# Decode attention mixed with a squared-ReLU MLP: TensorE's rounds 0 to 11 in one nest of two loops, the MLP's turn behind it, and a first w2 block loaded as 121 and 7 rows

## The chip, the cores and the metric

The kernel runs on one core of a Trainium2 chip. The metric is the device time of one execution in microseconds; lower is better. Engines are named as in the profile: PE is TensorE (PEld its weight loads), DVE VectorE, ACT ScalarE, POOL GpSimd, SP SyncE. SPq and ACTq are the instructions of SP and ACT that issue DMAs.

## What is computed

For two batch rows x (2 x 1 x 448) the program mixes an attention block over a long cache and an MLP by a learned gate. All arrays are float32.

```python
q = (x @ wq).reshape(B, Sq, H, Dh)              # H = 16 heads, Dh = 256
scores = einsum("bhqd,bhkd->bhqk", q, k_cache) * Dh ** -0.5     # Sk = 4096
a = (softmax(scores) @ v_cache).reshape(B, Sq, H * Dh) @ wo
h = x @ w1 + b1                                 # 448 -> 1792
b = relu(h) ** 2 @ w2 + b2                      # 1792 -> 448
g = sigmoid((x * gate_w).sum(-1))
out = g * a + (1 - g) * b
```

The two caches hold 2 x 16 x 4096 x 256 values each, 268 MB together, and every value is read once.

## The kernel before

**Rounds.** The work is cut into 16 rounds. A round i takes one batch row and two heads, so it loads 8,388,608 bytes of K and as many of V, each as a tile of 128 partitions by 64 x 256 values (partitions 0 to 63 one head, 64 to 127 the other). K alternates between two tiles, kp0 and kp1 (round i uses number i % 2). V has one tile, vp. In a round

- DVE multiplies the K tile in place by the query, half a tile at a time, and sums the rows (`times_q` L404 and `row_sums` L409, together `rest`, L413): four instructions;
- `maximum` (L420): DVE takes a maximum per partition (m), PE spreads it over the partitions by a matmul (mt), and DVE reduces that to the negated maximum per head (nb, L431, the first line of `softmax`);
- ACT writes the exponentials to pw and their sums to rs (L438);
- `values` (L466): PE multiplies pw by the V tile in 64 matmul instructions and accumulates in PSUM (po);
- `make_q` (L375) prepares a query two rounds ahead: PE spreads a row of qs, ACT copies it. `pick` (L383) has ACT choose the next row.

**Units.** Four rounds make a unit (L262). Behind units 0, 1 and 2 stand `sums` (L453, PE adds rs over partitions), `norm` (L458, three small DVE instructions), `turn_wide` (L483: twice two ACT copies that spread po four times, and 16 PE instructions), four ACT copies to oTw, and `project` (L521): PE multiplies oTw by the unit's 1.8 MB of wo, which `load_wo` fetched into the tile wo.

**Order.** The order on every engine is the order in which the program calls `op`; an instruction waits on semaphores for what it reads and overwrites (`Flow.op`, L46). Nothing overtakes on an engine. SP issues nearly all loads, in this order in the looped rounds: V of round i, K of round i + 2, and after each unit's last round wo. A load waits until the tile that it overwrites has been read, and SP waits with it. In rounds 0 to 11 PE's instructions are written as three loops of four passes, one for each unit (L573 to L597); since a loop's waits must be the same in each pass, they use tokens (`take`, `give`), semaphores that are counted down again. The end of each unit and rounds 12 to 15 are written out.

**After the loops** (L599 to L608) comes round 12 with the order changed: SP issues K of round 14, V of round 12, and, once DVE's `rest` of round 13 has read kp1, K of round 15. PE's `values` of round 12 stand behind `maximum` of round 13. V of round 13 waits for those. V of round 14 goes into kp0, V of round 15 into vp in three pieces, and then w2 into the low columns of kp1 in five pieces, cut at columns 2, 8, 11 and 13 of 14 (W2_CUTS, L192; `load_w2`, L540). The last w2 piece is the last load.

**The MLP.** x @ w1 is done at the start, into the PSUM bank ph; ACT copies it to the tile shared at once (L396). `ffn_turn` (L550, PE, 28 matmuls of 64 columns) and `ffn_square` (L557, five small DVE instructions) stand in round 0, the second behind DVE's `rest` of round 1. hT, their result, is used first at the very end (`late_w2`, L545).

Of the kernel before, what the change touches and what calls it, by code (L numbers as in the profile page):

```python
# [23 lines left out]
class Flow:  # L24
# [7 lines left out]
    def __init__(self, nc):  # L32
        self.nc = nc
        self.eng = {PE: nc.tensor, ACT: nc.scalar, DVE: nc.vector, POOL: nc.gpsimd, SP: nc.sync}
        self.order = {e: [] for e in self.eng}
        self.ops = {}
        self.know = {e: {} for e in self.eng}
        self.seen = {}
        self.tokens = {}
        self.body, self.at, self.passes = None, 0, 0  # L40

# [4 lines left out]
    def op(self, eng, fn, r=(), w=(), give=None, take=(), dma=None):  # L46
        proc = dma or eng
        looped = eng == PE and self.body is not None
        o = Op(proc, eng, fn, give, looped)
# [38 lines left out]
        if looped:  # L88
            if self.passes == 1:
                self.body.append(o)  # L90
            else:
                first = self.body[self.at]
# [11 lines left out]

    def loop(self):
        self.body, self.passes = [], 0

    def next_pass(self):
        assert self.passes < 2 or self.at == len(self.body)
        self.passes += 1  # L110
        self.at = 0

    def end_loop(self, slot=None):
        assert self.at == len(self.body)
        self.order[PE].append((self.passes, self.body, slot))
        self.body = None

    def emit(self):
# [36 lines left out]
        for eng in (POOL, DVE, ACT, SP, PE):  # L155
            for o in self.order[eng]:
                if isinstance(o, Op):
                    one(o)
                else:
                    passes, body, slot = o  # L160
                    with nc.Fori(0, passes, engines=bass.OrderedEngineSet([TYPES[PE]]),
                                 head_slot=None if slot is None else {TYPES[PE]: slot}):
                        for p in body:
                            one(p)
            if eng == SP:
                nums = sorted(s.num for s in sems.values())
                assert nums == list(range(nums[0], nums[0] + len(nums)))
                nc.sync.sem_clear(range(nums[0], nums[0] + len(nums)))


def gated_mix_kernel(nc, x, k_cache, v_cache, wq, wo, w1, b1, w2, b2, gate_w, out):
# [19 lines left out]
    DQ = D // 4  # L191
    W2_CUTS = (2, 8, 11, 13)  # L192
    V_CUTS = (32, 56)
    LEAD = 4
    HJ = HG * DH // P
# [23 lines left out]
    eo = sb("eo", P, 2)  # L219
    m16 = sb("m16", P, 4 * HG)  # L220
    xT = sb("xT", P, 2, XC, 2, B)
    z = sb("z", B, 1)
# [83 lines left out]
    def vec(fn, r, w, give=None):  # L306
# [12 lines left out]
    vec(lambda: v_.tensor_reduce(m16, ident.rearrange("p (r k) -> p k r", r=4)[:, :4 * HG, :], axis=AX.X, op=ALU.add),  # L319
        ["ident"], ["m16"])  # L320

    xr = start_at[:, 4 * D:].rearrange("b (k r s) -> b k r s", k=XC, s=2)
# [51 lines left out]
    def make_q(i, token=False):  # L374
        c = sel if token else col(i)  # L375
        op(PE, mms([(pq[k * PH:(k + 1) * PH, :DH], c.to_broadcast([P, PH]), qs[:, k * DH:(k + 1) * DH], True, True)
                    for k in range(2)]), r=["qs", "sel" if token else "ident"], w=["pq"], take=["q"] if token else ())
        t = q_t[i % 3]
        q_of[i] = t
        op(ACT, lambda: s_.activation(t, pq[:, :DH], AF.Copy), r=["pq"], w=[f"q{i % 3}"])  # L380

    def pick(i):
        c = col(i)  # L383
        op(ACT, lambda: s_.activation(sel, c, AF.Copy), r=["ident"], w=["sel"], give="q")

# [6 lines left out]

    h_sb = shared[:2 * B, :F // 2]
    op(PE, times_x(ph, w1_t, D, FB // 2), r=["xT", place(vp, 0, D * F // P)], w=["ph"])
    for k in range(FB // 2):
        op(ACT, lambda k=k: s_.activation(h_sb[:, k * D:(k + 1) * D], ph[32 * k:32 * k + 2 * B, :D], AF.Copy),  # L396
           r=["ph"], w=[("shared", k * D, (k + 1) * D)])
    load_k(1)
# [20 lines left out]
    def maximum(i, token=False):  # L419
        s = s_t[i % 2]  # L420
        vec(lambda: v_.tensor_reduce(m, s, axis=AX.X, op=ALU.max), [f"s{i % 2}"], ["m"], give="m" if token else None)
        op(PE, mms([(mt[k * PH:(k + 1) * PH, :PH], m.to_broadcast([P, PH]), ident[:, k * PH:(k + 1) * PH], True, True)
                    for k in range(2)]), r=["m", "ident"], w=["mt"], take=["m"] if token else ())

# [3 lines left out]
    def softmax(i):  # L428
        b, n = rounds[i]
        s, nb, rs, pw = s_t[i % 2], nb_t[i % 2], None, pwt[buf(i)]  # L430
        vec(lambda: v_.tensor_reduce(nb, mt[:, :PH], axis=AX.X, op=ALU.max, negate=True), ["mt"], [f"nb{i % 2}"])  # L431
        u, k = unit_of[2 * n]
        rs = rs_t[u % 2]

        def part(e):
# [3 lines left out]
                                          bias=nb[at], accum_out=rs[at, c:c + 1]),  # L439
               r=[f"s{i % 2}", f"nb{i % 2}"], w=[(f"pw{buf(i)}", 2 * c, 2 * c + 2), (f"rs{u % 2}", c, c + 1)],  # L440
               give="pw" if e and i < LOOPED else None)

# [3 lines left out]
    def clear(i):  # L446
# [4 lines left out]
           w=[("pw0", 2 * (B * (k + e) + b), 2 * (B * (k + e) + b) + 2) for e in range(2)])  # L451

    def sums(u):  # L453
        n = B * len(units[u])
        op(PE, mms([(sm[:, :n], ones_pp, rs_t[u % 2][:, :n], True, True)]), r=["ones", f"rs{u % 2}"], w=["sm"])

# [23 lines left out]

    o_w = shared.rearrange("r (s j k p) -> r s j k p", s=2, j=HJ // 2, k=HG)

    def turn_wide(u):  # L483
        ptv = sm[:, :HJ * HG * B].rearrange("p (j c) -> p j c", c=HG * B)
        po, rl = po_t[0], rl_t[u % 2]
        pv = po.rearrange("r (s p j) -> r s j p", s=2, j=HJ)
        for lo in range(0, HJ, HJ // 2):
            for s in range(2):
                op(ACT, lambda s=s, lo=lo: s_.activation(o_w[:, s], pv[:, s, lo:lo + HJ // 2].unsqueeze(2).to_broadcast([P, HJ // 2, HG, HP]),  # L489
                                              AF.Copy), r=["po0"], w=[("shared", s * HN // 2, (s + 1) * HN // 2)])  # L490
            ov = o_w.rearrange("r s j k p -> r s j (k p)")
            op(PE, mms([(ptv[:, lo + j, :], ov[:, s, j, :], rl[:, :, s], s == 0, s == 1)
                        for j in range(HJ // 2) for s in range(2)]), r=["shared", f"rl{u % 2}"], w=["sm"])
        if u < NG - 2:
            op(ACT, lambda: s_.activation(po, zero.to_broadcast([P, 512]), AF.Copy), r=["zero"], w=["po0"])
        for k in range(HG):
            at = slice(k * HP, (k + 1) * HP)
            op(ACT, lambda k=k, at=at: s_.activation(oTw[at], ptv[at, :, B * k:B * k + B], AF.Copy), r=["sm"], w=[("oTw", k, k + 1)])  # L498

# [15 lines left out]
    def load_wo(u):  # L515
        if u < NG - 1:
            load(SP, "wo", wo_t, wo_g[u], ["wo"])
# [172 lines left out]
```

## Time and profile before

| | |
|---|---|
| time, median of 3 runs | 677.68 us (677.6 to 677.97) |
| the profiled execution, time | 677.82 us |
| the profiled execution, span from first to last instruction | 676.5 us |
| mean granted clock of PE | 0.662 |
| DVE busy | 570.2 us (84%) |
| PE busy | 245.4 us (36%) |
| ACT busy | 42.3 us (6%) |
| read from HBM | 289.56 MB |
| DMA busy, each fortieth of the span but the last | 90% or more |

The profile is one execution. Its page gives each engine's busy time, a row of forty equal slices, the DMA queues, the chain of work that ended last, and the costliest groups of instructions with what ended the idle time in front of them. The timeline lists instructions with their start in us from the span's start, their duration, their engine, output and inputs, and, in brackets, how long the engine had been idle and what released it. 1.3 us of the measured time lie outside the span.

### The profile page before, as it was taken

The page shows a single profiled execution, that of the slowest core. Times are in us where ns is not written, and L with a number is a line of the kernel's source. Part 1 is how long each engine was busy: PE and PEld are TensorE (multiplying, and loading weights), DVE is VectorE, ACT ScalarE, POOL GpSimd, SP SyncE. Part 2 cuts the span into 40 slices and gives each one's busy share as a digit, 9 for nine tenths or more (in the row PEclk, how much of TensorE's full clock was granted, in tenths as well). Part 3 has the DMA queues.
Part 4 walks back from the last instruction along what each step waited for, and adds up shares of the span by engine and source line. Part 5 has one row for each costly group of instructions (what it writes and reads, how often), then busy time and mean ns, then how long its engine had stood idle before and what let it go on. Part 6 is the DMA issues. An engine that isn't in the chain of part 4 may idle for free.

```text
span 676.5 us, 3789 instructions
## 1 busy us (share of the span) xinstructions
PE 245.4 (36%) x1658; PEld 83.3 (12%) x1658; DVE 570.2 (84%) x143; ACT 42.3 (6%) x141; POOL 0.7 (0%) x6
## 2 busy tenths in 40 slices
PE   2522350502305761140505456050411580412476
PEld 1100210100001410010101411010100140100122
DVE  3069999999999895979979896897979899999920
ACT  0001000010100201010000201000010110000000
POOL 0000000000000000000000000000000000000000
PEclk9957585655758577585756678575665765675889
DMA  9999999999999999999999999999999999999997
GB/s 381 426 438 435 435 434 434 434 434 434 434 434 434 419 435 434 434 434 434 434 434 434 457 431 434 434 434 434 430 434 430 401 460 434 434 434 434 392 439 304
DMA packets 7062, 289.71 MB, mean 428 GB/s; under 512 B 902, under 2 KB 1036, under 8 KB 1932
## 3 DMA queue, kind: packets, MB, share of 16 engines
q1 hardware_dynamic: 6880, 289.54, 99.3%
q8 instruction: 8, 0.13, 0.1%
q10 hardware_dynamic: 172, 0.02, 0.0%
q14 instruction: 2, 0.02, 0.0%
HBM read 289.56 MB, written 0.01 MB: 428 GB/s over the span
## 4 chain that ended last, share of the span: by engine, by line
DMA 48%; DVE 31%; PE 3%; SPq 1%; issue 0%; DVEq 0%
DMA kp<-in_A_k_cache_dram 32%; DVE s L409 15%; DVE kp L404 15%; DMA vp<-in_A_v_cache_dram 11%; DMA kp<-in_B_w_dram 5%; PE po L333 3%; SPq L254 1%; PE fin L333 0%; PE mt L333 0%; DVE shared L660 0%; DVEq L147 0%; DVE nb L431 0%
## 5 line engine op out<-in xcount | busy, mean ns | idle before, releaser
L404 DVE TENSOR_TENSOR kp<-kp,q 128x8192 f32<-128x8192 f32 (+2 forms) x34 | 278.2, 8183 | 57.6 <-DMA kp<-in_A_k_cache_dram 57.6
L409 DVE TENSOR_REDUCE s<-kp 128x32 f32<-128x8192 f32 x32 | 278.0, 8686 | 1.1
L333 PE MATMUL po<-vp,pw 128*16 128x512 f32 (+1 forms) x960 | 135.8, 728 | 233.0 <-PEq L145 208.9
L333 PEld LDWEIGHTS po<-vp,pw 128*16 128x16 f32 (+1 forms) x960 | 31.1, 110 | 333.5 <-issue 307.3
L333 PE MATMUL mt<-ident,m 128*64 128x64 f32 x64 | 7.3, 318 | 141.3 <-PEq L145 87.4
L333 PE MATMUL sm<-rl,shared 128*128 128x8 f32 (+1 forms) x112 | 23.6, 347 | 9.2 <-ACT shared L489 8.1
L333 PE MATMUL acc<-wo,oTw 128*2 128x448 f32 x48 | 24.8, 683 | 2.5 <-ACT oTw L498 2.5
L333 PEld LDWEIGHTS sm<-rl,shared 128*128 128x128 f32 x112 | 23.0, 311 | 10.8 <-DVE rl L462 4.6
L450 ACT ACTIVATE pw<-zero 128x128 f32<-128x128 f32 x12 | 3.7, 312 | 325.5 <-PE po L333 325.5
L333 PEld LDWEIGHTS mt<-ident,m 128*64 128x64 f32 x64 | 4.8, 191 | 155.0 <-issue 99.0
L438 ACT ACTIVATE pw<-s,nb 64x64 f32<-64x64 f32 x32 | 11.1, 348 | 169.8 <-DVE nb L431 169.6
L660 DVE COPY shared<-fin 128x112 f32<-128x112 f32 x1 | 0.3, 275 | 20.8 <-PE fin L333 20.8
L333 PE MATMUL ph<-vp,xT 128*4 128x448 f32 x28 | 8.2, 759 | 15.6 <-DMA vp<-in_B_w_dram 15.6
L333 PE MATMUL po<-kp,pw 128*8 128x512 f32 x64 | 9.4, 744 | 8.8 <-DMA kp<-in_A_v_cache_dram 8.8
L333 PE MATMUL pq<-qs,sel 128*64 128x256 f32 x48 | 12.3, 594 | 0.0
L431 DVE TENSOR_REDUCE nb<-mt 128x1 f32<-128x64 f32 x16 | 3.6, 224 | 9.8 <-PE mt L333 9.8
L333 PE MATMUL po<-vp,xT 128*4 128x512 f32 x56 | 8.7, 787 | 4.9 <-DMA vp<-in_A_wq_dram 4.9
L460 DVE RECIPROCAL rc<-sm 128x8 f32<-128x8 f32 (+1 forms) x5 | 1.0, 196 | 7.7 <-PE sm L333 7.7
L380 ACT ACTIVATE q<-pq 128x256 f32<-128x256 f32 x16 | 6.1, 383 | 21.0 <-PE pq L333 20.7
L489 ACT ACTIVATE shared<-po 128x512 f32<-128x512 f32 x12 | 6.5, 591 | 11.4 <-PE sm L333 11.4
L333 PEld LDWEIGHTS acc<-wo,oTw 128*2 128x2 f32 x48 | 4.5, 98 | 20.6 <-issue 17.8
L438 ACT ACTIVATION_READ_ACCUMULATOR pw<-s,nb 64x1 f32 x32 | 5.9, 184 | 0.0
(65 smaller groups left out, 66.2 us busy)
## 6 DMA issues: line engine op xcount, KB each, us to landing
vp<-in_A_wq_dram SPq DMA_DIRECT2D x1, 7168.0 KB, 19.4
wo<-in_A_wo_dram SPq DMA_DIRECT2D x4, 1792.0 KB, 45.2
vp<-in_A_v_cache_dram SPq DMA_DIRECT2D x1, 4096.0 KB, 24.8
vp<-in_B_w_dram SPq DMA_DIRECT2D x1, 3136.0 KB, 18.0
vp<-in_A_v_cache_dram SPq DMA_DIRECT2D x1, 3072.0 KB, 31.7
kp<-in_B_w_dram SPq DMA_DIRECT2D x1, 1344.0 KB, 37.1
vp<-in_A_v_cache_dram SPq DMA_DIRECT2D x1, 1024.0 KB, 33.7
kp<-in_B_w_dram SPq DMA_DIRECT2D x2, 448.0 KB, 33.5
```

The lines of the kernel that those rows point to most:

```text
L254: op(eng, lambda: e.dma_start(dst, src), r=r, w=w, dma=sem, give=give)
L333: i = t_.matmul(out_, lhsT, rhs, start=start, stop=stop, skip_group_check=True)
L380: op(ACT, lambda: s_.activation(t, pq[:, :DH], AF.Copy), r=["pq"], w=[f"q{i % 3}"])
L404: vec(lambda: v_.tensor_tensor(kt, kt, q.unsqueeze(1).to_broadcast([P, hi - lo, DH]), op=ALU.mult), at + [f"q{i % 3}"], at)
L409: vec(lambda: v_.tensor_reduce(s[:, at], rows(t)[:, at, :], axis=AX.X, op=ALU.add), [place(t, half * HALF, (half + 1) * HALF)], [(f"s{i % ...
L431: vec(lambda: v_.tensor_reduce(nb, mt[:, :PH], axis=AX.X, op=ALU.max, negate=True), ["mt"], [f"nb{i % 2}"])
L438: op(ACT, lambda: s_.activation(pw[at, :, 2 * c:2 * c + 2], s[at].rearrange("p (m s) -> p m s", s=2), AF.Exp, bias=nb[at], accum_out=rs[at ...
L450: op(ACT, lambda: s_.activation(at, zero.unsqueeze(2).unsqueeze(3).to_broadcast([P, NK // 2, 2, 2]), AF.Copy), r=["zero"], w=[("pw0", 2 * ...
L460: vec(lambda: v_.reciprocal(c, sm[:, :B * n].rearrange("p (k b) -> p k b", b=B)), ["sm"], ["rc"])
L489: op(ACT, lambda s=s, lo=lo: s_.activation(o_w[:, s], pv[:, s, lo:lo + HJ // 2].unsqueeze(2).to_broadcast([P, HJ // 2, HG, HP]), AF.Copy), ...
L660: vec(lambda: v_.tensor_copy(y4, fin[:, :DQ]), ["fin"], [("shared", 0, DQ)])
```

## The change

The change replaces PE's three loops by one nest: an outer loop of three units, in it an inner loop of four rounds, then the end of the unit. So the end of a unit is now written once, and its waits have become tokens as well:

- `make_q` is one matmul of 128 columns instead of two of 64, with two ACT copies of 64 partitions instead of one of 128; `maximum` is one matmul instead of two, and `softmax` reduces mt in two DVE instructions of 64 partitions. The token for pw is now given by `pick`, behind the exponentials and the copies of q.
- `hold_sums` (new): ACT copies rs to rs_w before `sums` reads it.
- `norm_wide` (new) takes the place of `norm` for units 0 to 2: DVE also folds the two halves of po into a tile o (128 x 256) and works out rw from m8, a new constant.
- `turn_wide` has one ACT copy of 1024 columns and 8 matmuls, where it had four copies of 512 and 16 matmuls.
- `project` takes tokens of ACT's last copy to oTw and of wo's load.
- The MLP: ACT's copies of ph, `ffn_turn` and `ffn_square` are moved from the start and from rounds 0 and 1 to the place behind the nest, ahead of the loads and DVE's `rest` of round 13. ACT's two copies write each value twice, into the tile wo (it was the tile shared), and `ffn_turn` has 14 matmuls of 128 columns where it had 28 of 64.
- w2 is cut at columns 1, 8, 11 and 13, and the first piece is loaded as two, rows 0 to 120 and rows 121 to 127.

```diff
-    W2_CUTS = (2, 8, 11, 13)
+    W2_CUTS = (1, 8, 11, 13)
     V_CUTS = (32, 56)
+    LOW_ROWS = 121
...
     def make_q(i, token=False):
         c = sel if token else col(i)
-        op(PE, mms([(pq[k * PH:(k + 1) * PH, :DH], c.to_broadcast([P, PH]), qs[:, k * DH:(k + 1) * DH], True, True)
-                    for k in range(2)]), r=["qs", "sel" if token else "ident"], w=["pq"], take=["q"] if token else ())
+        op(PE, mms([(pq[:, :2 * DH], c.to_broadcast([P, P]), qs, True, True)]), r=["qs", "sel" if token else "ident"], w=["pq"])
...
-        op(ACT, lambda: s_.activation(t, pq[:, :DH], AF.Copy), r=["pq"], w=[f"q{i % 3}"])
+        for k in range(2):
+            at = slice(k * PH, (k + 1) * PH)
+            op(ACT, lambda k=k, at=at: s_.activation(t[at], pq[at, k * DH:(k + 1) * DH], AF.Copy), r=["pq"], w=[(f"q{i % 3}", k, k + 1)])
...
-    h_sb = shared[:2 * B, :F // 2]
     op(PE, times_x(ph, w1_t, D, FB // 2), r=["xT", place(vp, 0, D * F // P)], w=["ph"])
-    for k in range(FB // 2):
-        op(ACT, lambda k=k: s_.activation(h_sb[:, k * D:(k + 1) * D], ph[32 * k:32 * k + 2 * B, :D], AF.Copy),
-           r=["ph"], w=[("shared", k * D, (k + 1) * D)])
     load_k(1)
...
+    def norm_wide(u):
+        c = rc[:, :HG]
+        po = po_t[0]
+        vec(lambda: v_.reciprocal(c, sm[:, :B * HG].rearrange("p (k b) -> p k b", b=B)), ["sm"], ["rc"])
+        vec(lambda: v_.tensor_tensor(c, c, gP[:, 0, :].unsqueeze(1).to_broadcast([P, HG, B]), op=ALU.mult), ["rc", "gP"], ["rc"])
+        vec(lambda: v_.tensor_tensor(rw, m8, c.rearrange("p k b -> p (k b)"), op=ALU.mult), ["m8", "rc"], ["rw"])
+        vec(lambda: v_.tensor_scalar(o_t, po[:, :DH], eo[:, 0:1], None, op0=ALU.mult), ["po0", "eo"], ["o"])
+        vec(lambda: v_.scalar_tensor_tensor(o_t, po[:, DH:], eo[:, 1:2], o_t, op0=ALU.mult, op1=ALU.add), ["po0", "eo", "o"], ["o"])
...
+        op(ACT, lambda: s_.activation(o_w, o_t.rearrange("r (p j) -> r j p", j=HJ).unsqueeze(2).to_broadcast([P, HJ, HG, HP]),
+                                      AF.Copy), r=["o"], w=["shared"], give="turn")
+        ov = o_w.rearrange("r j k p -> r j (k p)")
+        op(PE, mms([(ptv[:, j, :], ov[:, j, :], rw, True, True) for j in range(HJ)]), r=["shared", "rw"], w=["sm"], take=["turn"])
...
         op(PE, mms([(acc[:B, :D], oTw[:, j, :], t[:, j, :], False, u == NG - 2 and j == HJ - 1) for j in range(HJ)]),
-           r=["oTw", "wo"], w=["acc"])
+           r=["oTw", "wo"], w=["acc"], take=["oT", "wo"])
...
         for lo, hi in zip(at, at[1:]):
-            load(SP, f"w2_{lo}", w2_t[:, lo:hi, :], w2_v[:, lo:hi, :], [place(kp[last % 2], lo * D, hi * D)])
+            if lo:
+                load(SP, f"w2_{lo}", w2_t[:, lo:hi, :], w2_v[:, lo:hi, :], [place(kp[last % 2], lo * D, hi * D)])
+                continue
+            for a, b in ((0, LOW_ROWS), (LOW_ROWS, P)):
+                load(SP, f"w2_{lo}_{a}", w2_t[a:b, lo:hi, :], w2_v[a:b, lo:hi, :], [place(kp[last % 2], lo * D + a, lo * D + b)])
...
     def ffn_turn():
-        hv = h_sb.rearrange("r (p c) -> r c p", c=FC)
+        h_sb = wo_t[:2 * B, :F]
+        hv = h_sb.rearrange("r (a k n) -> r k a n", a=2, k=FB // 2)
+        for k in range(FB // 2):
+            op(ACT, lambda k=k: s_.activation(hv[:, k], ph[32 * k:32 * k + 2 * B, :D].unsqueeze(1).to_broadcast([2 * B, 2, D]), AF.Copy),
+               r=["ph"], w=["wo"])
+        hc = h_sb.rearrange("r (m c) -> r c m", c=FC)
         pt = sm[:, :FC * 2 * B].rearrange("p (c r) -> p c r", r=2 * B)
-        op(PE, mms([(pt[a * PH:(a + 1) * PH, c, :], hv[:, c, :], ident[:2 * B, :2 * B], True, True)
-                    for c in range(FC) for a in range(2)]), r=["shared", "ident"], w=["sm"])
+        op(PE, mms([(pt[:, c, :], hc[:, c, :], ident[:2 * B, :2 * B], True, True) for c in range(FC)]), r=["wo", "ident"], w=["sm"])
         return pt
...
-    pt = ffn_turn()
     make_q(2)
     pick(3)
 
+    flow.nest()
     for i in range(LOOPED):
-        if i % HG == 0:
-            flow.loop()
-        flow.next_pass()
+        flow.enter("inner")
         vt = load_v(i, vp)
         load_k(i + 2)
         values(i, vt)
         clear(i)
         rest(i + 1, 0, 0)
-        if i == 0:
-            ffn_square(pt)
         if i % HG == HG - 1:
             load_wo(i // HG)
         maximum(i + 1, True)
         softmax(i + 1)
+        if (i + 1) % HG == HG - 1:
+            hold_sums()
         make_q(i + 3, True)
         if i < LOOPED - 1:
             pick(i + 4)
         if i % HG == HG - 1:
+            flow.enter("outer")
             u = i // HG
-            flow.end_loop(16 * u)
             sums(u)
-            norm(u)
+            norm_wide(u)
             turn_wide(u)
             project(u)
+    flow.end_nest(NG - 1, HG, 39)
+    pt = ffn_turn()
+    ffn_square(pt)
 
     i = last - 3
     load_k(i + 2)
```

More of the change, by code (lines that the diff above doesn't have):

```diff
@@ L39, in __init__ @@
         self.tokens = {}
-        self.body, self.at, self.passes = None, 0, 0
+        self.parts, self.part, self.at = None, None, 0
     @staticmethod
@@ L47, in op @@
         proc = dma or eng
-        looped = eng == PE and self.body is not None
+        looped = eng == PE and self.part is not None
         o = Op(proc, eng, fn, give, looped)
@@ L88, in op @@
         if looped:
-            if self.passes == 1:
-                self.body.append(o)
+            if self.at is None:
+                self.parts[self.part].append(o)
             else:
-                first = self.body[self.at]
+                first = self.parts[self.part][self.at]
                 assert first.takes == o.takes and not o.waits, (first.takes, o.takes)
@@ L103, in learn, with nest, enter, leave @@
         know[p.proc] = max(know.get(p.proc, 0), p.n)
[L105 to L116, printed above, removed]
+    def nest(self):
+        self.parts = {}
+    def enter(self, part):
+        self.leave()
+        self.part, self.at = part, 0 if part in self.parts else None
+        self.parts.setdefault(part, [])
+    def leave(self):
+        assert self.part is None or self.at in (None, len(self.parts[self.part]))
+        self.part = None
+    def end_nest(self, outer, inner, slot):
+        self.leave()
+        self.order[PE].append((outer, inner, self.parts["inner"], self.parts["outer"], slot))
     def emit(self):
@@ L159, in emit @@
                 else:
[L160 to L163, printed above, removed]
+                    outer, inner, body, rest, slot = o
+                    engines = bass.OrderedEngineSet([TYPES[PE]])
+                    with nc.Fori(0, outer, engines=engines, head_slot={TYPES[PE]: slot}):
+                        with nc.Fori(0, inner, engines=engines):
+                            for p in body:
+                                one(p)
+                        for p in rest:
                             one(p)
@@ L220, in gated_mix_kernel @@
     m16 = sb("m16", P, 4 * HG)
+    m8 = sb("m8", P, 2 * HG)
+    rw = sb("rw", P, 2 * HG)
+    o_t = sb("o", P, DH)
+    rs_w = sb("rs_w", P, B * HG)
     xT = sb("xT", P, 2, XC, 2, B)
@@ L375, in make_q @@
         c = sel if token else col(i)
-        op(PE, mms([(pq[k * PH:(k + 1) * PH, :DH], c.to_broadcast([P, PH]), qs[:, k * DH:(k + 1) * DH], True, True)
-                    for k in range(2)]), r=["qs", "sel" if token else "ident"], w=["pq"], take=["q"] if token else ())
+        op(PE, mms([(pq[:, :2 * DH], c.to_broadcast([P, P]), qs, True, True)]), r=["qs", "sel" if token else "ident"], w=["pq"])
         t = q_t[i % 3]
         q_of[i] = t
-        op(ACT, lambda: s_.activation(t, pq[:, :DH], AF.Copy), r=["pq"], w=[f"q{i % 3}"])
+        for k in range(2):
+            at = slice(k * PH, (k + 1) * PH)
+            op(ACT, lambda k=k, at=at: s_.activation(t[at], pq[at, k * DH:(k + 1) * DH], AF.Copy), r=["pq"], w=[(f"q{i % 3}", k, k + 1)])
     def pick(i):
         c = col(i)
-        op(ACT, lambda: s_.activation(sel, c, AF.Copy), r=["ident"], w=["sel"], give="q")
+        op(ACT, lambda: s_.activation(sel, c, AF.Copy), r=["ident"], w=["sel"], give="pw")
     op(PE, times_x(po_t[1], wq_t, QB, NQ // 2), r=["xT", place(vp, 0, D * N // P)], w=["po1"])
@@ L421, in maximum @@
         vec(lambda: v_.tensor_reduce(m, s, axis=AX.X, op=ALU.max), [f"s{i % 2}"], ["m"], give="m" if token else None)
-        op(PE, mms([(mt[k * PH:(k + 1) * PH, :PH], m.to_broadcast([P, PH]), ident[:, k * PH:(k + 1) * PH], True, True)
-                    for k in range(2)]), r=["m", "ident"], w=["mt"], take=["m"] if token else ())
+        op(PE, mms([(mt[:, :P], m.to_broadcast([P, P]), ident, True, True)]), r=["m", "ident"], w=["mt"], take=["m"] if token else ())
     def buf(i):
@@ L430, in softmax @@
         s, nb, rs, pw = s_t[i % 2], nb_t[i % 2], None, pwt[buf(i)]
-        vec(lambda: v_.tensor_reduce(nb, mt[:, :PH], axis=AX.X, op=ALU.max, negate=True), ["mt"], [f"nb{i % 2}"])
+        for k in range(2):
+            at = slice(k * PH, (k + 1) * PH)
+            vec(lambda at=at: v_.tensor_reduce(nb[at], mt[at, at], axis=AX.X, op=ALU.max, negate=True), ["mt"], [(f"nb{i % 2}", at.start, at.stop)])
         u, k = unit_of[2 * n]
-        rs = rs_t[u % 2]
+        rn = u % 2 if u > NG - 2 else 0
+        rs = rs_t[rn]
         def part(e):
@@ L451, in clear, with hold_sums @@
            w=[("pw0", 2 * (B * (k + e) + b), 2 * (B * (k + e) + b) + 2) for e in range(2)])
+    def hold_sums():
+        op(ACT, lambda: s_.activation(rs_w, rs_t[0], AF.Copy), r=["rs0"], w=["rs_w"])
     def sums(u):
         n = B * len(units[u])
-        op(PE, mms([(sm[:, :n], ones_pp, rs_t[u % 2][:, :n], True, True)]), r=["ones", f"rs{u % 2}"], w=["sm"])
+        rs, name = (rs_t[u % 2], f"rs{u % 2}") if u > NG - 2 else (rs_w, "rs_w")
+        op(PE, mms([(sm[:, :n], ones_pp, rs[:, :n], True, True)]), r=["ones", name], w=["sm"])
     def norm(u):
@@ L494, in turn_wide @@
+        ov = o_w.rearrange("r j k p -> r j (k p)")
+        op(PE, mms([(ptv[:, j, :], ov[:, j, :], rw, True, True) for j in range(HJ)]), r=["shared", "rw"], w=["sm"], take=["turn"])
         if u < NG - 2:
-            op(ACT, lambda: s_.activation(po, zero.to_broadcast([P, 512]), AF.Copy), r=["zero"], w=["po0"])
+            op(ACT, lambda: s_.activation(po_t[0], zero.to_broadcast([P, 512]), AF.Copy), r=["zero"], w=["po0"])
         for k in range(HG):
             at = slice(k * HP, (k + 1) * HP)
-            op(ACT, lambda k=k, at=at: s_.activation(oTw[at], ptv[at, :, B * k:B * k + B], AF.Copy), r=["sm"], w=[("oTw", k, k + 1)])
+            op(ACT, lambda k=k, at=at: s_.activation(oTw[at], ptv[at, :, B * k:B * k + B], AF.Copy), r=["sm"], w=[("oTw", k, k + 1)],
+               give="oT" if k == HG - 1 else None)
@@ L516, in load_wo @@
         if u < NG - 1:
-            load(SP, "wo", wo_t, wo_g[u], ["wo"])
+            load(SP, "wo_given", wo_t, wo_g[u], ["wo"], give="wo")
         else:
```

15 lines of the change are left out of this document (3 added, 12 removed).

## The prediction

> **What bounds the kernel now.** I read the page first: span, DMA rows, costliest groups.
>
> ```profile
> span 676.5 us, 3789 instructions
> ...
> PE 245.4 (36%) x1658; PEld 83.3 (12%) x1658; DVE 570.2 (84%) x143; ACT 42.3 (6%) x141; POOL 0.7 (0%) x6
> ...
> GB/s 381 426 438 435 435 434 434 434 434 434 434 434 434 419 435 434 434 434 434 434 434 434 457 431 434 434 434 434 430 434 430 401 460 434 434 434 434 392 439 304
> ...
> q1 hardware_dynamic: 6880, 289.54, 99.3%
> q8 instruction: 8, 0.13, 0.1%
> ...
> L404 DVE TENSOR_TENSOR kp<-kp,q 128x8192 f32<-128x8192 f32 (+2 forms) x34 | 278.2, 8183 | 57.6 <-DMA kp<-in_A_k_cache_dram 57.6
> ```
>
> Queue q1, which carries the loads, uses 99.3% of what 16 DMA engines have in the span, at 434 GB/s in nearly every slice. DVE is idle only because K has not landed (57.6 us). So the loads are one stream without a hole, and a change moves the end in two ways: by its bytes and their order, or by letting the stream run dry. A load is issued when the tile that it overwrites has been read; the stream runs dry when that happens later than the end of what is queued. So I looked for the slack at the place where the change adds a wait, in the timeline behind the loops.
>
> ```profile
> 537.16 0.33 SPq L254 DMA_DIRECT2D kp<-in_A_k_cache_dram  x1
> ...
> 537.53 0.43 SPq L254 DMA_DIRECT2D vp<-in_A_v_cache_dram  x1
> ...
> 541.02 8.69 DVE L404 TENSOR_TENSOR kp<-kp,q 128x8192 f32<-128x8192 f32 x1 [0.97 <-DMA kp<-in_A_k_cache_dram]
> ...
> 575.78 0.33 SPq L254 DMA_DIRECT2D kp<-in_A_k_cache_dram  x1
> ...
> 584.04 9.25 PE L333 MATMUL po<-vp,pw 128*8 128x512 f32 x64 [7.49 <-DMA vp<-in_A_v_cache_dram]
> ```
>
> K of round 14 and V of round 12 are issued at 537.2 and 537.5. DVE starts round 13's `rest` at 541.0, as soon as K of round 13 has landed, and ends 34.8 us later; at that moment, 575.8, SP issues K of round 15 into the same tile. V of round 12, the last load queued ahead of it, lands at 584.0 (it releases PE). **The slack is 584.0 - 575.8 = 8.2 us**: if DVE began this `rest` more than that later, past 549.2, nothing would be queued.
>
> **The change part by part.** *The MLP behind the nest* is the part that counts. `ffn_square` now stands on DVE ahead of round 13's `rest`. It waits for `ffn_turn` on PE, which stands behind `project` of unit 2 and reads what ACT writes into the wo tile, which ACT may do only when that `project` has read it. Behind DVE's waiting instruction is the `rest` that frees kp1; on SP behind K of round 15 stand V of rounds 13, 14 and 15, wo and w2; on PE behind `ffn_turn` stand `maximum` of round 13 and `values` of round 12. So DVE, which before had only `norm` here, now waits for the whole end of the unit. The rows for that chain, from the timeline and from the groups by form:
>
> ```profile
> 539.43 0.21 DVE L460 RECIPROCAL rc<-sm 128x8 f32<-128x8 f32 x1 [1.16 <-PE sm L333]
> ...
> 539.87 0.18 DVE L462 TENSOR_TENSOR rl<-m,rc 128x16 f32<-128x16 f32 x1
> ...
> 540.72 3.55 PE L333 MATMUL sm<-rl,shared 128*128 128x8 f32 x16 [1.32 <-ACT shared L489]
> ...
> 549.12 0.73 ACT L498 ACTIVATE oTw<-sm 32x16 f32<-32x16 f32 x4 [3.67 <-PE sm L333]
> ...
> 549.91 8.38 PE L333 MATMUL acc<-wo,oTw 128*2 128x448 f32 x16 [0.82 <-ACT oTw L498]
> ...
> 551.36 0.13 PEld L333 LDWEIGHTS acc<-wo,oTw 128*2 128x2 f32 x1 [0.62 <-issue]
> 552.10 0.13 PEld L333 LDWEIGHTS acc<-wo,oTw 128*2 128x2 f32 x1 [0.62 <-issue]
> ...
> 557.00 0.09 PEld L333 LDWEIGHTS acc<-wo,oTw 128*2 128x2 f32 x1 [0.29 <-issue]
> 557.38 0.09 PEld L333 LDWEIGHTS acc<-wo,oTw 128*2 128x2 f32 x1 [0.29 <-issue]
> ```
> ```profile
> L380 ACT ACTIVATE q<-pq 128x256 f32<-128x256 f32 x16 | 6.1, 383 | 21.0 <-PE pq L333 20.7
> L489 ACT ACTIVATE shared<-po 128x512 f32<-128x512 f32 x12 | 6.5, 591 | 11.4 <-PE sm L333 11.4
> L396 ACT ACTIVATE shared<-ph 4x448 f32<-4x448 f32 x2 | 1.1, 534 | 23.4 <-PE ph L333 23.4
> L431 DVE TENSOR_REDUCE nb<-mt 128x1 f32<-128x64 f32 x16 | 3.6, 224 | 9.8 <-PE mt L333 9.8
> L354 DVE SCALAR_TENSOR_TENSOR kp<-kp 2x448 f32<-2x448 f32 x1 | 0.6, 611 | 2.2 <-DMA kp<-in_gate_w_dram 2.2
> L333 PE MATMUL sm<-ident,shared 4*64 4x4 f32 x56 | 3.6, 260 | 0.0
> L333 PE MATMUL pq<-qs,sel 128*64 128x256 f32 x48 | 12.3, 594 | 0.0
> ```
>
> - `sums` releases the reciprocal at 539.4 before. `make_q`, ahead of it on PE, becomes two instructions of 512 columns. `project`'s instructions of 448 columns follow each other every 0.75 us (551.36 to 552.10) and later every 0.38 us, so 512 columns take about 0.85 at the slow pace, 1.7 for two, where four at once took about 1.1. I take 0.6 more: 540.0.
> - `norm_wide`: three small DVE instructions as now (539.43 to 540.05, 0.6 us) and two of 256 columns, not in this trace. 64 columns take 0.224 and 448 take 0.611, 1.0 ns a column, so about 0.42 each, as an estimate: 541.5.
> - ACT's one copy of 1024 columns: 256 take 0.383 and 512 take 0.591, 0.81 ns a column, so 1.0: 542.5.
> - The turn: 16 instructions once (3.55 us), not twice: 546.1. ACT's four copies, until PE goes on (549.12 to 549.91): 0.8, 546.9.
> - `project`: 8.4 as now, 555.3. Ends: 16 instructions at 0.38 are 6.1, at 0.75 they are 12.0.
> - ACT's copies of ph: 448 columns took 0.534, 896 would take 0.9, two 1.8: 557.1.
> - `ffn_turn`: 28 instructions with weights of 128 columns. Half of the 3.6 us of the 56 with 64 columns would be 1.8; at the turn's rate (3.55 for 16) 28 are 6.2. The weight load is as wide as the turn's, so I take 4.9, nearer to that row: 562.0.
> - `ffn_square` 1.0 by its rows below, and, as an estimate, 0.4 for five handovers (ACT's last oTw copy ends at 549.85, 0.06 before PE starts): **DVE begins round 13's `rest` at 563.4 instead of 541.0**, 14.2 us past 549.2.
>
> wo of unit 2 has to be there for `project` (timeline, and the DMA issues of 498 to 500), and `ffn_square`'s own rows are those of round 1:
>
> ```profile
> 498.82 0.43 SPq L254 DMA_DIRECT2D wo<-in_A_wo_dram  x1
> ```
> ```profile
> wo<-in_A_wo_dram SPq DMA_DIRECT2D x1, 1792.0 KB, 46.5
> ```
> ```profile
> 109.97 0.37 DVE L560 TENSOR_TENSOR hb<-sm,b1T 64x28 f32<-64x28 f32 x2
> ...
> 110.82 0.19 DVE L564 TENSOR_TENSOR hT<-hT,gP 128x28 f32<-128x28 f32 x1
> ```
>
> It is issued at 498.8 and lands 46.5 us later, at 545.3, ahead of 546.9: no wait, but no `project` before 545.3 either. Five instructions from 109.97 to 111.01 are the 1.0 us of `ffn_square`; before, that lay in a stretch where the stream had enough queued, so its leaving there gains nothing.
>
> How late K of round 15 then lands, by the DMA issues of the page and of the stretch 575 to 577:
>
> ```profile
> vp<-in_A_wq_dram SPq DMA_DIRECT2D x1, 7168.0 KB, 19.4
> ```
> ```profile
> kp<-in_A_k_cache_dram SPq DMA_DIRECT2D x1, 27.6
> ```
>
> Now: 575.8 + 27.6 = 603.4. Then: 563.4 + 34.8 = 598.2 for the issue, into an empty queue. The one load issued into an empty queue, wq, took 19.4 us for 7168 KB; K has 8192 KB, so 2.4 more at 434 GB/s: 21.8, landing at 620.0. **The stream is 620.0 - 603.4 = 16.6 us late**, 14.2 of it dry and 2.4 the start of a transfer.
>
> *What lies beside other work.* The second nb instruction is 0.22 of DVE a round, the two instructions of `norm_wide` 0.84 a unit, `hold_sums` and the second copy of q some 0.2 to 0.4 of ACT (6% busy), all in rounds where DVE waits 57.6 us in total for K. If that cover were gone, 12 rounds and two units would cost DVE 4.3 us. The pw token now waits for the q copies as well: PE's `values` wait for V longer anyway. m8 is one small instruction at the start, where DVE waits for the first K. The shorter turn in units 0 and 1 shortens nothing, since PE waits for V behind it.
>
> *Fetches and the first w2 piece.*
>
> ```profile
> kp<-in_B_w_dram SPq DMA_DIRECT2D x1, 224.0 KB, 32.1
> ```
>
> A w2 column of 224 KB is 0.53 us of the stream; new cuts only shift which DMA engine carries how much of it. Eight fetches moved 0.13 MB, 16 KB each; on one engine, a sixteenth of 434 GB/s, that is 0.6 us. Three fewer save between nothing (different engines, none the last) and 1.8 us (all on the last engine). The two together: -2.3 to +0.3, and I take **-0.5**, near the lower gain, since the fetches are few and spread over the span. The Trainium skill, DMA: Bandwidth & Descriptors, section "Why a DMA increments its semaphore by 16 and not by 1", says that a load uses the largest number of engines up to 16 that divides its rows: 11 for 121 rows, 7 for 7, so five engines are spared. By that the end comes 0.5 us earlier if those five are the late ones and 0.3 later if they aren't; no row here shows single engines.
>
> **The sum.** The profiled execution took 677.8 (span 676.5, 1.3 around it), 0.1 above the median of 677.68. 677.8 + 16.6 - 0.5 = **693.9 us**.
>
> **What is late next.** DVE is 22.4 us late from 563.4 on, the stream 16.6, so what DVE feeds has 5.8 us less.
>
> ```profile
> 610.88 0.33 SPq L254 DMA_DIRECT2D kp<-in_A_v_cache_dram  x1
> ...
> 646.47 0.22 DVE L421 TENSOR_REDUCE m<-s 128x1 f32<-128x64 f32 x1
> ...
> 656.32 5.32 PE L333 MATMUL po<-vp,pw 128*8 128x512 f32 x32 [3.53 <-DMA vp<-in_A_v_cache_dram]
> ...
> 667.24 0.57 PE L333 MATMUL fin<-kp,hT 128*2 128x112 f32 x16
> ```
>
> V of round 14 would be issued at 633.3 with V of round 13 landing near 639: it holds. The last maximum would be at 668.9. PE was then busy until 652.8 (3.53 before 656.32), 6.3 us behind that maximum; the same gives 675.2, while the first piece of V of round 15 is there at 672.9 (656.3 + 16.6). PE would start the last values some 2 us behind their V, and can regain that before the last w2 piece, which it waited for between 667.2 and the end.
>
> **The rivals.**
>
> - *The chain is hidden* (not slower). If `ffn_square` is done by 549.2, or DVE goes on without it, the slack covers it and only the fetches and the cut are left: 677.3, at best 675.5. Against it: wo alone lands at 545.3, and `project` at its fastest pace takes 6.1. 6 in 100, mostly for my having read the order wrongly.
> - *PE sets the end.* It starts the last values 2.3 us late; if it also runs those 64 instructions at a pace like that of the first half (5.32 for 32), it ends behind w2, by some 2 us: 696. 8 in 100.
> - *The nest fetches again.* If the jump back over the outer loop, or the way out of it, makes PE wait for code, units 0 and 1 hide it (PE waits there for V), but the way out lies on the chain. q8's 0.1% of 16 engines' span is some 11 us, 1.4 a fetch: 695.3. 6 in 100, since the loops of before ran 12 rounds with 8 fetches in all. The Trainium skill, Runtime: NRT & Kernel Launch, section "Instruction fetch mechanics", speaks for it: a taken branch to a target outside the current window stalls on a fetch.
> - *The forecast*: 80 in 100.
>
> **The numbers.** The ends of the chain: 557.4 (`project` 2.3 shorter, `ffn_turn` 3.1, `make_q` 0.6) gives 10.6 us, 568.3 (3.6 and 1.3 longer) gives 21.5. With the ends of the last term the time lies between 686.1 and 699.6; all ends at one side are unlikely, and PE at the end adds some: 688 to 700. Within 0.2% (1.4 us) is about what a measurement here can't tell from no change. Slower by more: 0.94; same 0.04; faster 0.02, the last two from the first rival.
>
> **What would show it.** Right: DVE idle for over 20 us behind 541, released by PE's sm, just ahead of `ffn_square`; K of round 15 issued near 598; one or two slices of the GB/s row far below 434; five q8 packets. Wrong: `rest` of round 13 starting at 541, or K of round 15 issued before V of round 12 has landed.

## The result, and the profile after

| | before | after |
|---|---|---|
| time, median of 5 runs | 677.79 us (677.6 to 677.97) | 699.56 us (698.18 to 701.1) |
| ratio to before | | 1.0323, 95% interval 1.0309 to 1.0337 |
| the profiled execution, time | 677.82 us | 701.1 us |
| its span | 676.5 us | 699.8 us |

The change costs 21.8 us, 3.2%. The profiled execution after is the slowest of its five; its span is 23.3 us longer than the one before. The rows of its page that answer to those shown of before:

```profile
span 699.8 us, 3526 instructions
...
GB/s 414 426 424 420 431 465 420 420 424 450 443 423 416 461 427 423 420 468 423 427 420 452 428 423 438 450 427 423 420 468 395 442 457 82 240 431 458 389 439 253
...
q1 hardware_dynamic: 6882, 289.54, 96.2%
q8 instruction: 5, 0.08, 0.0%
...
L587 DVE TENSOR_TENSOR hb<-sm,b1T 64x28 f32<-64x28 f32 x2 | 0.4, 184 | 24.3 <-PE sm L345 24.3
```

The same 289.54 MB pass through q1, and two slices fall out, 82 and 240 GB/s in the 34th and 35th. That is one hole, not a slower stream: V of round 12, the last load ahead of it, lands at 584.0 in both kernels. The group at L587 is `ffn_square`'s first instruction: DVE stood idle 24.3 us in front of it, released by PE's sm. The timeline there:

```profile
540.05 0.21 DVE L500 RECIPROCAL rc<-sm 128x8 f32<-128x8 f32 x1 [1.46 <-PE sm L345]
...
541.10 0.48 DVE L504 SCALAR_TENSOR_TENSOR o<-po,eo,o 128x256 f32<-128x256 f32 x1
541.62 2.04 ACT L508 ACTIVATE shared<-o 128x1024 f32<-128x1024 f32 x1 [1.02 <-DVE o L504]
543.80 3.55 PE L345 MATMUL sm<-rw,shared 128*128 128x8 f32 x16 [3.78 <-PEq L148]
...
548.41 8.52 PE L345 MATMUL acc<-wo,oTw 128*2 128x448 f32 x16 [1.06 <-PEq L148]
...
556.98 1.84 ACT L577 ACTIVATE wo<-ph 4x896 f32<-4x896 f32 x2 [8.86 <-PE acc L345]
558.87 6.97 PE L345 MATMUL sm<-ident,wo 4*128 4x4 f32 x28 [1.94 <-ACT wo L577]
565.88 0.38 DVE L587 TENSOR_TENSOR hb<-sm,b1T 64x28 f32<-64x28 f32 x2 [24.30 <-PE sm L345]
...
566.84 8.69 DVE L413 TENSOR_TENSOR kp<-kp,q 128x8192 f32<-128x8192 f32 x1
...
601.59 0.33 SPq L265 DMA_DIRECT2D kp<-in_A_k_cache_dram  x1
```

Each row waits for the one above it or for a short one left out between them (PEq, PE's sequencer, takes the tokens that ACT gives), down to DVE's `rest` of round 13 at 566.8. 34.8 us later, at 601.6, K of round 15 is issued, 17.6 us after V of round 12 had landed. The DMA issues of that stretch give its landing:

```profile
kp<-in_A_k_cache_dram SPq DMA_DIRECT2D x1, 21.9
```

601.6 + 21.9 = 623.5, against 603.4 before: **20.1 of the 23.3 us**. The end, from the chain of work that ended last (start, duration, what):

```profile
655.91 0.37 SPq L265
...
660.50 32.55 DMA kp<-in_B_w_dram
693.05 0.04 issue
693.09 4.38 PE fin L345 x104
...
697.49 0.28 DVE shared L688
```

The w2 piece of seven columns lands at 693.05, and PE multiplies the last 104 instructions in one go; by the trace the three pieces behind it land by 696.3 meanwhile. So the remaining 3.2 us arise behind round 15's K: the last landing comes 72.9 us behind that K where it was 70.4, and PE ends 1.1 us behind it, not 0.4. The last stretch of both kernels, after first, then before (start and end, length, then busy time and count of PE, PEld, DVE, ACT and POOL, PE's granted clock, DMA):

```profile
693.00:697.50 4.50, 4.32 (x104) 3.36 (x104) 0.01 (x1) 0.00 (x0) 0.00 (x0) 0.62 0.30 112
```
```profile
670.00:674.20 4.20, 3.28 (x112) 2.02 (x100) 0.00 (x0) 0.00 (x0) 0.00 (x0) 1.00 0.57 223
```

The granted clock was 0.62 in the one and 1.00 in the other: 104 instructions took 42 ns each, where 112 took 29. Why less was granted is not shown.

### The profile page after: what moved, and what is told of

Read it like the earlier page. It is cut to its first block, busy times and chain, and to the rows that moved or that the text cites. A ratio compares the mean times of both kernels' runs of the same rounds, so it can differ in the third digit from the quotient of the medians.

```text
span 699.8 us, 3526 instructions
## 1 busy us (share of the span) xinstructions
PE 254.9 (36%) x1518; PEld 83.7 (12%) x1518; DVE 577.2 (82%) x166; ACT 49.4 (7%) x151; POOL 0.7 (0%) x6
## 3 DMA queue, kind: packets, MB, share of 16 engines
q1 hardware_dynamic: 6882, 289.54, 96.2%
## 5 line engine op out<-in xcount | busy, mean ns | idle before, releaser
L345 PE MATMUL mt<-ident,m 128*128 128x128 f32 x32 | 12.1, 479 | 178.0 <-PEq L148 92.8
L345 PEld LDWEIGHTS mt<-ident,m 128*128 128x128 f32 x32 | 7.8, 303 | 191.3 <-issue 103.5
L345 PE MATMUL pq<-qs,sel 128*128 128x512 f32 x24 | 22.1, 1022 | 0.0
L587 DVE TENSOR_TENSOR hb<-sm,b1T 64x28 f32<-64x28 f32 x2 | 0.4, 184 | 24.3 <-PE sm L345 24.3
L441 DVE TENSOR_REDUCE nb<-mt 64x1 f32<-64x64 f32 x32 | 7.1, 222 | 13.4 <-PE mt L345 12.9
L345 PE MATMUL sm<-rw,shared 128*128 128x8 f32 x48 | 10.7, 360 | 11.4 <-PEq L148 11.4
L345 PE MATMUL po<-kp,pw 128*8 128x512 f32 x64 | 11.1, 859 | 8.5 <-DMA kp<-in_A_v_cache_dram 8.5
L393 ACT ACTIVATE q<-pq 64x256 f32<-64x256 f32 x32 | 12.1, 378 | 17.9 <-PE pq L345 17.7
L345 PEld LDWEIGHTS sm<-rw,shared 128*128 128x128 f32 x48 | 10.5, 330 | 11.6 <-issue 11.6
L345 PE MATMUL sm<-ident,wo 4*128 4x4 f32 x28 | 7.0, 380 | 1.9 <-ACT wo L577 1.9
L345 PEld LDWEIGHTS sm<-ident,wo 4*128 4x128 f32 x28 | 6.9, 336 | 2.8 <-ACT wo L577 2.8
```

The source lines that it names most:

```text
L345: i = t_.matmul(out_, lhsT, rhs, start=start, stop=stop, skip_group_check=True)
L393: op(ACT, lambda k=k, at=at: s_.activation(t[at], pq[at, k * DH:(k + 1) * DH], AF.Copy), r=["pq"], w=[(f"q{i % 3}", k, k + 1)])
L441: vec(lambda at=at: v_.tensor_reduce(nb[at], mt[at, at], axis=AX.X, op=ALU.max, negate=True), ["mt"], [(f"nb{i % 2}", at.start, at.stop)])
L587: vec(lambda a=a, at=at: v_.tensor_tensor(hb[at], pt[at, :, a * B:(a + 1) * B], b1T[at].unsqueeze(2).to_broadcast([PH, FC, B]), op=ALU.add ...
```

## The experiments

The theory: DVE's wait holds back its `rest`, so a tile is freed too late and the stream of loads runs dry. The rivals: the nest with its tokens and fetches costs the time; the uneven w2 loads cost it; DVE's or PE's work is late in itself. Times are medians; beside each stands that of the kernel before, timed anew with it.

**1. ffn_square behind rest** (label e1_square_late), the changed kernel with

```diff
     pt = ffn_turn()
-    ffn_square(pt)
...
     rest(i + 1, 0, 0)
     load_k(i + 3)
+    ffn_square(pt)
```

> The changed kernel, with ffn_square alone moved on DVE from ahead of round 13's rest to behind it; the nest, ffn_turn on PE and the cut of w2 stay. Theory (DVE's wait lets the stream of loads run dry): rest starts again at 541 to 543, K of round 15 is issued before 580, time 677.0 to 678.0. Rival (the nest itself, its tokens or fetches, cost the time): 690 or more. Second rival (the loads of 121 and 7 rows, which use few DMA engines, cost some us at the end): 679 to 682.

679.27 us beside 678.0: ratio 1.0017, 1.0008 to 1.0026. Moving five instructions of 1 us in all gave back 20 us. DVE and SP in its timeline:

```profile
541.20 8.68 DVE L413 TENSOR_TENSOR kp<-kp,q 128x8192 f32<-128x8192 f32 x1
...
557.91 6.97 PE L345 MATMUL sm<-ident,wo 4*128 4x4 f32 x28 [1.94 <-ACT wo L577]
...
575.84 0.37 DVE L587 TENSOR_TENSOR hb<-sm,b1T 64x28 f32<-64x28 f32 x2
575.95 0.33 SPq L265 DMA_DIRECT2D kp<-in_A_k_cache_dram  x1
```

`ffn_turn` takes as long as in the changed kernel and ends nearly as late (564.9, there 565.8), but nobody waits for it: DVE is in the middle of `rest`. K of round 15 is issued at 575.95. The first rival falls. 1.3 us remain above before, more than the theory allowed and just inside the second rival's range.

**2. The MLP alone** (e2_mlp_alone): the kernel before, three loops, old cut, and

```diff
-    pt = ffn_turn()
     make_q(2)
...
-        if i == 0:
-            ffn_square(pt)
...
             project(u)
+    pt = ffn_turn()
+    ffn_square(pt)
```

with the changed kernel's `ffn_turn`, ACT's copies of ph included.

> The kernel before with the MLP part of the change alone: ACT's copies into the wo tile, ffn_turn and ffn_square behind the loops. Theory: project of unit 2 ends at 558.3 as before, then 1.84 for ACT's copies, 6.97 for ffn_turn and 1.1 for ffn_square, so rest starts at 568.3 and the time is 677.8 + 568.3 - 546.8 = 699.3, plus up to 2. Rival (the nest costs the time): 677 to 679.

700.58 beside 678.0: ratio 1.0335, 1.032 to 1.0351. The move alone makes the whole loss, with eight fetches and the old cut.

```profile
559.34 6.97 PE L333 MATMUL sm<-ident,wo 4*128 4x4 f32 x28 [1.94 <-ACT wo L550]
566.35 0.38 DVE L560 TENSOR_TENSOR hb<-sm,b1T 64x28 f32<-64x28 f32 x2 [26.34 <-PE sm L333]
...
567.32 8.68 DVE L400 TENSOR_TENSOR kp<-kp,q 128x8192 f32<-128x8192 f32 x1
...
602.07 0.33 SPq L254 DMA_DIRECT2D kp<-in_A_k_cache_dram  x1
```

**3. The same as 1 with w2 cut as before** (e3_late_old_cut):

```diff
-    W2_CUTS = (1, 8, 11, 13)
+    W2_CUTS = (2, 8, 11, 13)
...
-            for a, b in ((0, LOW_ROWS), (LOW_ROWS, P)):
-                load(SP, f"w2_{lo}_{a}", ...)
+            load(SP, f"w2_{lo}", ...)
```

> The changed kernel with ffn_square behind rest, and w2 cut as before (2, 8, 11, 13, whole rows). Theory: no dry stream, 677.3 to 678.3; the difference to the same kernel with the new cut is what the cut is worth, forecast 0.5 us in favour of the new cut, bounds 0.5 either way. Rival (few DMA engines at the end cost us): 2 us or more faster than with the new cut.

677.75 beside 678.0: ratio 0.9998, 0.9989 to 1.0007. The nest, with five fetches for eight, is worth nothing that can be measured. The 1.3 us of experiment 1 belong to the cut, and they are a loss.

**4. The cut alone** (e4_cut_alone): the kernel before with the changed W2_CUTS and the loads of 121 and 7 rows.

> The kernel before with the new cut of w2 alone (first column as 121 and 7 rows). Theory: within 0.5 us of before, 677.3 to 678.3. Rival (few DMA engines at the end cost us): 679 to 682.

679.29 beside 678.0: ratio 1.0021, 1.0011 to 1.003. The sign of the forecast was wrong; the rival's range holds it, at its lower edge.

**5. The new cut with whole rows** (c1_whole_rows): the kernel before with `W2_CUTS = (1, 8, 11, 13)` and nothing else.

> The kernel before with w2 cut at columns 1, 8, 11, 13, the first column in one load of 128 rows. If the split of the rows made the 1.3 us that the new cut costs: 678.0, as before. If the shorter first piece made them: 679.3.

677.96 beside 678.05: ratio 1.0, 0.999 to 1.0009. Not the place of the cut, then: the split of the rows.

**6. 112 and 16 rows** (c2_112_16): experiment 4 with

```diff
-    LOW_ROWS = 121
+    LOW_ROWS = 112
```

> The kernel before with the new cut of w2, but the first column's rows as 112 and 16, both multiples of 16. If the cost comes from the uneven share (a load of 121 rows on fewer DMA engines, so that these carry more): 678.0. If any split of the rows, which gives the engines other rows than the loads around it, costs it: 679.3.

679.18 beside 678.05: ratio 1.002, 1.0011 to 1.003. The cost is that of 121 and 7 within 0.2 us. The Trainium skill, DMA: Bandwidth & Descriptors, section "Why a DMA increments its semaphore by 16 and not by 1", gives 112 and 16 rows all 16 engines, and 121 and 7 rows 11 and 7 of them. The traces agree: as its data land the semaphore of the load of 121 rows is raised 11 times and that of 7 rows 7 times, after one early step each, and those of 112 and 16 rows 16 times each. So a smaller number of engines is not what costs.

**7. The first column in two halves of its width** (c3_column_halves): again a load more, with pieces half as long, but 128 rows in each. Against experiment 4's kernel:

```diff
-            for a, b in ((0, LOW_ROWS), (LOW_ROWS, P)):
-                load(SP, f"w2_{lo}_{a}", w2_t[a:b, lo:hi, :], w2_v[a:b, lo:hi, :], ...)
+            for a, b in ((0, D // 2), (D // 2, D)):
+                load(SP, f"w2_{lo}_{a}", w2_t[:, lo:hi, a:b], w2_v[:, lo:hi, a:b], ...)
```

> The kernel before with w2 cut at columns 1, 8, 11, 13 and the first column in two loads of 128 rows, each half as wide (896 bytes a row). If what costs is that a DMA engine writes other rows than in the loads around it: 678.0. If it is a further load with short pieces: 679 to 679.3.

678.24 beside 677.89: ratio 1.0004, 0.9995 to 1.0013. Neither the further load nor the short piece makes the 1.3 us; the split by rows does. Why is not shown: that each DMA engine then has other rows than in the loads around it fits all four runs, but no run shows which rows an engine takes. The Trainium skill, on the same page in the section "The descriptor swizzle", says that in a load of 128 partitions each engine writes the partitions of one port; a split by rows would break that and one by columns would not, which agrees, and no run here shows a port.

**8 to 10. A dose of delay** (d1_4096, d2_8192, d3_16384): the kernel before with one DVE instruction put behind `project` of unit 2, ahead of `rest`, n = 4096, 8192 or 16384:

```diff
+    vec(lambda: v_.tensor_reduce(dly, kp[1][:, :n], axis=AX.X, op=ALU.max), [place(kp[1], 0, n)], ["dly"])
 
     i = last - 3
```

> The kernel before with a DVE reduction of 4096 columns of kp1, 4.4 us, ahead of round 13's rest. rest starts at 545.4, K of round 15 is issued at 580.2, 3.8 before the landing of V of round 12, so more than the 2.4 of a transfer's start. Theory (slack): no change, 677.7 to 678.5. Rival (DVE's work moves the end one for one): 682.4.

> The kernel before with one DVE reduction of 8192 columns of kp1, 8.7 us, put ahead of round 13's rest (it adds work whose result is used nowhere). rest starts at 549.7, K of round 15 is issued at 584.5, 0.5 behind the landing of V of round 12. Theory (a dry stream costs its gap and 2.4 us for the start of a transfer): 680.7. Rival (the gap alone): 678.3. Rival (DVE's work moves the end one for one): 686.5.

> The same with a reduction of 16384 columns, 17.4 us. rest starts at 558.4, the issue comes at 593.2, 9.2 behind the landing. Theory: 677.8 + 9.2 + 2.4 = 689.4, up to 2 more at the end. Rival (the gap alone): 687.0. Rival (one for one): 695.2.

| n | delay of `rest`, us | K of round 15 issued | time | beside | ratio, interval |
|---|---|---|---|---|---|
| 4096 | 4.4 | 580.14 | 678.24 | 677.89 | 1.0006, 0.9997 to 1.0015 |
| 8192 | 8.5 | 584.25 | 682.54 | 678.05 | 1.0067, 1.0048 to 1.0086 |
| 16384 | 17.1 | 592.92 | 690.48 | 678.05 | 1.0184, 1.0165 to 1.0203 |

The issues of the three kernels, in this order, from their timelines of SP:

```profile
580.14 0.33 SPq L255 DMA_DIRECT2D kp<-in_A_k_cache_dram  x1
```
```profile
584.25 0.33 SPq L255 DMA_DIRECT2D kp<-in_A_k_cache_dram  x1
```
```profile
592.92 0.33 SPq L255 DMA_DIRECT2D kp<-in_A_k_cache_dram  x1
```

4.4 us of delay are free, 17.1 cost 12.4: a slack, and behind it nearly one for one. One for one from zero is out. From the second to the third dose (two runs each) the issue moves by 8.7 and the time by 7.9. But both cost more than gap and start, 4.5 where 2.9 was forecast and 12.4 where 11.6, and up to 2 more at the end, was.

**11. The late load in halves** (e5_split_k15), the changed kernel with

```diff
     rest(i + 1, 0, 0)
-    load_k(i + 3)
+    load_k(i + 3, 0, J)
+    load_k(i + 3, J, NK)
```

> The changed kernel, with K of round 15 loaded in two halves, so that the first half needs only the first half of round 13's rest. Theory: the first half is issued at 566.8 + 17.4 = 584.2 and streams from 586.6 to 596.3, the second is issued at 601.6 and lands at 613.8 instead of 623.5: the time is 9.7 us less, 689.9. Rival (the time is lost to DVE's lateness behind this point, not to the late load): 698 to 700.

696.86 beside 677.89: ratio 1.0276, 1.0261 to 1.0292; 2.7 us below the changed kernel, not 9.7. The first half goes out at 583.8 as expected, and by the trace V of round 13 lands at 633.6, 9.3 us earlier than in the changed kernel. But then DVE and PE, and SP, in its timeline:

```profile
628.00 8.69 DVE L418 TENSOR_REDUCE s<-kp 128x32 f32<-128x8192 f32 x1
...
659.85 6.16 PE L345 MATMUL po<-kp,pw 128*8 128x512 f32 x32 [11.52 <-DMA kp<-in_A_v_cache_dram]
```
```profile
636.71 0.33 SPq L265 DMA_DIRECT2D kp<-in_A_v_cache_dram  x1
```

V of round 14 overwrites kp0, which DVE's `rest` of round 14 has read only at 636.7, 3.1 us behind that landing. The stream, dry between the two halves too (595.8 to 601.1), ran dry once more, and V of round 14 landed at 659.8 (it releases PE), 26.2 us behind V of round 13 where 19.4 is its time in the stream. So 6.8 of the 9.7 us went at once into the next late tile. The rival, DVE's lateness behind this point, has its share here.

**12. The changed kernel with the old cut** (a1_old_cut): the edit of experiment 3 on the changed kernel.

> The changed kernel with w2 cut as before. If the split rows cost their 1.3 us behind a dry stream as well: 698.3. If the dry stream or PE at the end hides them: 699.6.

698.69 beside 677.89: ratio 1.0305, 1.0291 to 1.0319. The changed kernel's own ratio is 1.0323, 1.0309 to 1.0337; the intervals overlap, so that the split costs 1 us here too is likely and not settled. The two traces point the same way: from the issue of round 15's K to the last landing it is 94.8 us in the changed kernel and 93.5 here.

No kernel here beats the one before: experiments 3, 5, 7 and 8 are equal to it.

## Why the prediction was right, and where its sizes were off

The mechanism was right, step by step, and so was its place. The time is 5.7 us above the forecast of 693.9 and 0.4 below the upper end of the range; the slowest of the five runs, 701.1, lies above it. All the larger misses went upward, so that the time still fell inside is partly luck. The terms:

- *The chain.* `sums` released the reciprocal at 540.05 (540.0 forecast) and `norm_wide` ended at 541.6 (541.5). **ACT's copy of 1024 columns took 2.04 us, not 1.0**: the step that carried 0.81 ns a column over from copies out of PSUM failed; this one reads SBUF. `project` took 8.52 (8.4), ACT's copies of ph 1.84 (1.8). **`ffn_turn` took 6.97, not 4.9**, and more than the end of 6.2 taken from the turn's rate: 0.25 us for each of 28, not 0.22. The half of the old rate, the other end, had no bearing. `rest` began at 566.8, 3.4 later than forecast, and these two terms make 3.1 of that.
- *From `rest` to K's landing*: 34.8 and 21.9 us, as worked out (34.8 and 21.8). Experiments 9, 10 and 12 repeat it, 21.8 to 22.0 from issue to landing; experiment 2 does not, 23.05.
- *The slack* of 8.2 us holds in the main: 4.4 us are free (experiment 8), and 8.5, 0.3 past it, cost 4.5 (experiment 9). But its last part is not free. In experiment 11 the first half of K is issued 0.45 us before V of round 12 lands (583.82 and 584.27), and it lands 11.5 us behind it, where 4096 KB take 9.7 at 434 GB/s. So a tile has to be released some time before the queue ends; in experiment 8 it was 4.0 us before, and nothing was lost.
- *Fetches and the first w2 piece*: forecast -0.5. Five q8 packets came as expected, each of 0.9 to 1.1 us, between the 0.6 and the 1.4 worked out; but the nest is worth nothing measurable (experiment 3) and the split of the rows costs 1.2 us (experiments 4 to 7). The step that failed counted only bytes for each engine; its bounds, -2.3 to +0.3, did not hold the 1.2.
- *Behind round 15's K*: forecast as before, measured 2.5 us later at the last landing. Some 1.2 can be the split. The rest shows with the old cut too: in experiments 9, 10 and 12 the last landing is 72.1, 71.5 and 71.8 us behind that K, against 70.4 (in experiment 2 it is 70.5, behind a K that landed 1.1 later). A reading, which no run tested by itself, is in the trace's increments of the last load's semaphore, taken here as one for each DMA engine (dose 16384 is experiment 10):

```
before       672.02 672.06 672.08 672.09 672.15 672.24 672.26 672.70 673.00 673.28 673.40 673.47 673.48 673.56 673.65 673.72
dose 16384   684.73 684.79 684.81 684.86 684.89 684.92 684.93 684.93 685.05 685.09 685.11 685.24 685.25 685.29 686.31 686.43
```

Before, nine engines trail the other seven by up to 1.7 us, which code fetches spread over the whole span would explain. In the hole all engines wait for the same issue and start level; the two that trail by 1.1 us at the end would be those that a fetch has met since. By this reading the lateness gathered before the hole is forgiven, and what is lost behind it counts in full.

The traces fit it in two more places. The 16 increments of round 15's K lie within 0.7 us in the changed kernel, where before they are spread over 1.8. And in each of the six kernels with a hole (the changed one and experiments 2, 9, 10, 11 and 12) two packets of q8, the queue of the code fetches, of 0.9 to 1.1 us each, come between K's issue and the last stretch, and two increments trail at the end; a third packet comes only 1.6 to 2.3 us before the last landing. In experiment 2 the first of them (613.5) falls into K's own transfer, and one increment of K comes 1.3 us behind the other fifteen, which would explain its 23.05.

- *The rivals.* The chain was not hidden. PE was late by 4 us for the last values (681.4, where V's first piece had landed at 677.4; 2.3 forecast) and had regained it when V's last piece came, for which it waited 0.5 us; what it added at the end, 0.7 us, fits the granted clock of its last 104 instructions (0.62): in experiment 12, at 1.00, it ended 0.4 us behind the last landing, as before. No wait for code shows on the way out of the nest: in the changed kernel ACT starts its copies 0.05 us behind `project`, and PE starts `ffn_turn` 0.05 behind those; a fetch inside the 1.9 us for which PE waits there would not show. The Trainium skill's sentence on taken branches (Runtime: NRT & Kernel Launch, section "Instruction fetch mechanics") found no case here: five fetches served twelve rounds and three turns of the outer loop.

## What to carry to other kernels

A small instruction that moves to another place takes its wait along, and everything behind it on its engine waits too: look first at what the next instruction there sets free. In a kernel whose loads form one stream, ask of each tile how long before the end of the queue it is released; a delay well within that slack is free (here 4.4 of 8.2 us), one near its end already costs part of a transfer's start, and beyond it a delay costs its length and that start. A repair of one such place can move the loss to the next tile (6.8 of 9.7 us in experiment 11) when the late engine itself is not relieved.

## What the runs showed of the hardware that was not expected

- A load of 224 KB ahead of the last ones, split by rows (121 and 7, or 112 and 16), cost 1.1 to 1.5 us (experiments 4 and 6, and 1 less 3); split by columns with all 128 rows in each, nothing measurable (0.3 us, interval -0.3 to 0.9).
- ACT's copy of 1024 columns out of SBUF took 2.04 us, 2.0 ns a column, where its copies of 512 out of PSUM took 0.591, 1.2 ns a column. Both read with a stride and write each value four times; what makes the difference was not tried.
- 28 matmul instructions with weights of 4 rows by 128 columns took 6.97 us (0.25 each) in three kernels alike (the changed one and experiments 1 and 2), at granted clocks of 0.58, 0.53 and 0.51, although each multiplies by 4 columns only.
- A K load of 8192 KB issued into an empty queue took 21.8 to 22.0 us to land in four kernels and 23.05 in one, in which a q8 packet falls into that stretch; in the stream a load of that size takes 19.4 (V of rounds 13 and 14 before).
- A load of 121 rows raised its semaphore 11 times as its data landed, one of 7 rows 7 times, and loads of 112, 16 and 128 rows 16 times each.
